# A fused gated-attention and MoE kernel: Q's transposed steps regrouped in runs of 16, masks and output rows to match, and one load untied from the weight conversions

## The chip, the cores and the metric

The kernel runs on one core of one Trainium2 chip. Its time is device microseconds of one launch, from a few runs; smaller is better. The times here are the median of three runs, and the profile is of one further execution.

## The reference

```python
def _attn_ref(q, k, v, a_re, a_im):            # each (B, H, S, D) = (4, 8, 768, 48), float32
    mag = np.sqrt(a_re * a_re + a_im * a_im)
    scale = np.minimum(mag, 0.999) / (mag + 1e-06)
    a_re_n, a_im_n = (a_re * scale, a_im * scale)
    for t in range(S):                         # S_re, S_im: (B, H, D, D), zero at first
        ar, ai = (a_re_n[:, :, t, :, None], a_im_n[:, :, t, :, None])
        new_re = ar * S_re - ai * S_im
        new_im = ar * S_im + ai * S_re
        kv = np.einsum('bhd,bhde->bhde', k[:, :, t], v[:, :, t])   # outer product of k and v
        S_re, S_im = (new_re + kv, new_im)
        y[:, :, t] = np.einsum('bhd,bhde->bhe', q[:, :, t], S_re)

def _moe_ref(x, w_in, w_out):                  # w_in (384, 2048), w_out (2048, 384)
    h = x @ w_in
    r = np.maximum(h, 0.0)
    return ((r * r) @ w_out).astype(np.float32)

# x = y as (B*S, H*D) = (3072, 384); the output is (3072, 384) float32
```

A recurrence with a complex decay for each channel runs along S for each of 32 heads. Its output, with the 8 heads side by side, goes through a two-layer block with a squared relu.

## The kernel before, in words

**Units.** The 4 x 768 tokens are cut into NU = 6 units of L = 512 tokens, each in W = 4 chunks of C = 128 tokens. In a unit the 8 heads are 4 pairs; tile halves z = 0 and 1 hold two pairs each (`aq[z]`, `ff[z]`). The complex values of one head are R = 96 rows, cut in NJ = 3 blocks of 32. In the natural layout partition p holds the four steps 4p to 4p+3 of its chunk, "c" being the step mod 4.

**What a unit does.** `load` (L882, SP's queue, and L896 for v on POOL's) brings a_re, a_im, then q and k. The chain (L913 to L1197: logarithms and roots on ACT from L918 and L926, normalisation on DVE at L929 to L950, running products at L968 and L976, totals over partitions by PE at L997, then the decays applied to q and k at L1155 to L1193) leaves decayed Q and K in `ff[z]`. `gather` (L1230) copies K in natural layout to KC for the state update. For each pair, `turn` (unit 2 on, EARLY = 2) transposes Q and K: two DVE 32x32 block transposes of 128x768 (L1266) write into `aq[z]`, and 12 DMAs (L1271, 8 on SP's queue, 4 on ACT's) move 32-row blocks to the tile QT, where the 96 rows are on partitions. In units 0 and 1 `turn_pe` (L1289) does it with PE and ACT instead. Then come `score` (PE L1314, and DVE L1317 multiplies by the causal mask), `keep` (PE L1343, DVE L1357: the state), `mix` (PE L1369 and L1373 into the accumulator yp, ACT L1381 copies to yt, five DMAs per two pairs at L1388 put yt into xT, the 384 rows of the MoE's input).

**The dense part.** L1410 multiplies xT by w_in, ACT squares the relu (L1441, L1442) or DVE does half of it (L1522), and L1456 (unit 0) or L1507 (later units) multiplies by w_out. L1531 moves the result to the tile `ot`, and `rows` (L1468) writes 128 rows of 384 with one DMA, on POOL's queue, but on SP's for the last two blocks of the last unit.

**Weights.** Both weight matrices arrive as 64-bit patterns in 8 + 8 pieces (`fetch`, L799 on POOL's queue) and are turned into float32 by `convert`: L813 and L817 on ACT, L819, L823 and L826 on DVE. Pieces 3 to 7 of w_in carry the extra key ("a", 1) among the first DVE step's reads.

**Order of the work.** Every operation is a step in the class `Plan` with an engine, a duration written by hand, keys that it reads and writes, and a rank. `Plan.order` schedules the steps in a list over these durations (ready steps first by rank: chain of the next unit, pairs, conversions, dense), and emits them in the order of their planned starts. Each engine and each DMA queue then runs its own instructions strictly in this order. A key that a step reads makes later writers of that key wait for it, too; so the load that next writes ("a", 1), unit 1's second a, is ordered behind those w_in conversions. In the trace the w2 matmuls of the unit before serve as filler among a unit's pairs, and behind a unit's last mix stand those w1 matmuls that need only xT's first rows. The planner's set of engines is iterated in an order that can differ between builds, so that builds of one file can differ in the order of a few steps of unit 0 and 1.

The layout that the change is about: in QT the columns of Q and K are written with

```python
dst = T6[:, i % 2].rearrange("p j (k h t c) -> p k c h j t", k=2, h=2, c=W)
```

so that column t*4 + c is step 4t + c: order of time, every write 4 elements from the one before. `score` and `mix` read and write with matching views.

Of the kernel before, what the change touches and what calls it, by code (L numbers as in the profile page):

```python
# [598 lines left out]
def fast_path(ctx, tc, q, k, v, a_re, a_im, moe_w_in, moe_w_out, out, flag):  # L599
# [98 lines left out]
    for o in range(2):  # L698
        for p0 in (0, CH):
            part = mask[p0:p0 + CH, ts(o, C)]  # L700
            pool.affine_select(out=part, in_=part, pattern=[[1, C]], compare_op=ALU.is_ge,
                               fill=0.0, base=-(p0 ^ (CH * o)), channel_multiplier=-1)
    mask4 = mask.rearrange("p (o t) -> p o t", o=2).unsqueeze(1).to_broadcast([C, W // 2, 2, C])
    dve.memset(ypair, 0.0)
    for b in ("sc0", "sc1"):
        dve.memset(bank[b], 0.0)
# [93 lines left out]
            (CONV, i), 2 * PW * 4 * C, 4.0)  # L800

    def convert(i):
        held = [("a", 1)] if SOON <= i < NPIECE else []
        _, t, keys, dst, n, wk = piece(i)
        t3 = t.rearrange("p m (f two) -> p m f two", two=2)
        lo, hi = t3[:, :, :, 0], t3[:, :, :, 1]
        bits = dst.bitcast(U32)
        rank = (W2, 0.6) if i >= NPIECE else (W1, 0.3)
        def part(dtype, i):
            return t.bitcast(dtype).rearrange("p m (f four) -> p m f four", four=4)[:, :, :, i]  # L810

# [14 lines left out]
        step("DVE", tt(PW), keys + [("lo", i, int(mixed))], wk, lambda: dve.tensor_tensor(  # L826
            out=bits, in0=bits, in1=lo, op=ALU.add), rank)
# [38 lines left out]
    def load(n):  # L866
# [23 lines left out]
        for i in range(W):  # L890
            b, s = divmod(n * L + i * C, S)
            src = v[b, :, s:s + C, :].rearrange("h t d -> t h d")
            for p0, t0, m in places(i):
                vrank = (CHAIN, 1) if n == 1 else (DENSE, 6 + n)
                dma(pool, [("xT", (n - (vs(n) == vs(n - 1))) % 2, NM - 1)] if n else [("gate",)], [("v", vs(n))],
                    lambda i=i, p0=p0, t0=t0, m=m, src=src: pool.dma_start(  # L896
                        out=t[p0:p0 + m, i], in_=src[t0:t0 + m]), vrank, m * 1536, 4.0,
                    group=n)

# [318 lines left out]
    def gather(n, z, p, np):  # L1218
# [5 lines left out]
        for i in needs(n):  # L1224
            for p0, t0, m in places(i):
                queue = sp if n < EARLY and i % 2 else pool
                t0, m4 = 32 * i + t0 // W, m // W
                dma(queue, keys, [(k_, z, q_) for q_ in range(p, p + np)
                                  for k_ in ("KC", "KC%d" % (i == 3))],
                    lambda i=i, p0=p0, t0=t0, m=m, m4=m4, queue=queue: queue.dma_start(  # L1230
                        out=kc[p0:p0 + m, i], in_=nat[t0:t0 + m4]),
                    rank, m * w * 4, group=(n, p))

    slot = {"tr": 0, "sc": 0, "A": 0, "St": 0, "yt": 0, "QT": 0, "d": 0, "ot": 0, "g": 0}
    trs = ["tr0", "tr1"]
# [6 lines left out]
    def pairs(n, which):  # L1244
# [9 lines left out]
        def turn(i):  # L1254
# [2 lines left out]
            t = QT[s].rearrange("p (i x) -> p i x", i=W)  # L1257
            got["T", i] = s
            T6 = aq[z].rearrange("p (y j x) -> p y j x", y=2, j=NJ)
            for j in range(2):  # L1260
                nat = ff[z][:, j * Z:(j + 1) * Z].rearrange(
                    "p (c h j r) -> p c h j r", c=W, h=HH, j=NJ)[:, :, ts(i % 2, 2)]
                dst = T6[:, i % 2].rearrange("p j (k h t c) -> p k c h j t", k=2, h=2, c=W)
                step("DVE", 1.39, [("f", z, 2 * j), ("f", z, 2 * j + 1)],
                     [("a", z) if i % 2 == 0 else ("qk", z)],
                     lambda nat=nat, dst=dst, j=j: dve.transpose(out=dst[:, j], in_=nat), rank)  # L1266
            for b in range(W):
                for j in range(NJ):
                    queue = act if j == 2 else sp
# [26 lines left out]
        def columns(s):  # L1296
            t6 = QT[s].rearrange("p (i k h %s) -> p i k h t c" % "t c",
                                 i=W, k=2, h=2, c=W)[0:R]
            return t6[:, :, 0], QT[s].rearrange("p (i k h t) -> p i k h t", i=W, k=2, h=2)[0:R, :, 1]

        def score(i, h):
            s = got["T", i]
            qt, kt = columns(s)
            b = "sc%d" % take("sc", 2)
            sa = bank[b].rearrange("p (j t c) -> p j t c", j=W, c=W)
# [11 lines left out]
            step("DVE", tt(L), [(b,)], [("A", a)], lambda: dve.tensor_tensor(  # L1317
                out=As[a].rearrange("p (j o t) -> p j o t", o=2, t=C),
                in0=bank[b].rearrange("p (j o t) -> p j o t", o=2, t=C), in1=mask4,
                op=ALU.mult), rank)  # L1320

        def keep(i):
# [35 lines left out]
                                 out=o, in0=ps[:, j], in1=at[j], op=ALU.add), rank)  # L1358

        def mix(i):  # L1360
            qt, _ = columns(got["T", i])
            y4 = ypair.rearrange("p (j t c) -> p j t c", j=W, c=W)
            at, s = got["S", i]
            aa = [As[got["A", i, h]].rearrange("p (j t) -> p j t", j=W) for h in range(2)]

            def go():
                for j in range(W):
# [2 lines left out]
                                  rhs=aa[h][:, j], start=True, stop=at[j] is None)  # L1370
                    for h in range(2):
                        if at[j] is not None:
                            pe.matmul(y4[64 * h:64 * h + D, j], lhsT=at[j][:, h],  # L1373
                                      rhs=qt[:, j, h], start=False, stop=True)
# [90 lines left out]
    def rows(n, grp, i, o):  # L1465
        r = n * L + (2 * grp + i) * C
        queue = sp if n == NU - 1 and grp == 1 else pool
        dma(queue, [("ot", o, 0), ("ot", o, 1)], [], lambda: queue.dma_start(  # L1468
            out=out[r:r + C, :], in_=ots[o]), (DENSE, n), C * DM * 4)

# [226 lines left out]
```

## Time and profile before

| what | us |
|---|---|
| median of 3 runs | 700.21 |
| lowest, highest run | 698.01, 701.38 |
| the profiled execution | 699.64 |
| its span | 697.9 |
| outside the span | 1.74 |

The profile is a page and a trace of one execution. PE is TensorE's matmuls, PEld its weight loads, DVE, ACT, POOL and SP the other engines; a "q" behind a name is that engine's DMA queue or sequencer. A row of a timeline reads: start in us, duration, engine, line of the kernel, operation, output <- inputs, shape, how many merged; in brackets, the idle time of that engine just before and what ended it. Where rows merge several instructions, the duration is from the start of the first to the end of the last. A row of the page's groups reads: busy us and mean ns of one, then idle time before. A row of DMA issues ends with KB and the median us from issue to landing. One L1410 product of 128x512 in the accumulators is 2 x 3 matmuls of 128x256.

### The profile page before, as it was taken

The numbers are of one execution on the slowest core, as the hardware profiler recorded it, in microseconds if no ns is written. First come the engines' busy times: TensorE is split into PE (matmuls) and PEld (weight loads), VectorE is DVE, ScalarE is ACT, GpSimd is POOL, SyncE is SP. The second block draws the span as 40 slices with busy tenths as digits, with TensorE's granted clock in tenths as the row PEclk, the third lists the DMA queues.
The fourth block names the chain that finished last, engine by engine and source line by source line (L and its number), as shares of the span: only waits on it lengthen the run. The fifth ranks groups of instructions, "written<-read, shape, count | busy, mean of one in ns | idle before, by whom it ended". The sixth has DMA issues, their size and how long they took to land.

```text
span 697.9 us, 11865 instructions
## 1 busy us (share of the span) xinstructions
PE 628.0 (90%) x4442; PEld 558.0 (80%) x4442; DVE 559.1 (80%) x1125; ACT 341.6 (49%) x586; POOL 96.4 (14%) x166
## 2 busy tenths in 40 slices
PE   0117999899999999998999999999999999999996
PEld 0006777586788999987998998998999989989996
DVE  6999994789879799676998798998897999428631
ACT  6688727955675163335544436444357351032230
POOL 6301140021100002020021030011030011032200
PEclk9999899999999999999999999999999999999999
DMA  9924278021440005745027662036560034368600
GB/s 282 336 104 98 64 174 255 3 66 28 138 141 13 12 12 127 187 115 117 2 68 169 153 142 60 1 85 177 136 163 10 23 88 113 93 221 302 249 3 27
DMA packets 52067, 79.53 MB, mean 114 GB/s; under 512 B 7744, under 2 KB 35072, under 8 KB 52000
## 3 DMA queue, kind: packets, MB, share of 16 engines
q0 software_dynamic: 11712, 40.90, 19.4%
q1 hardware_dynamic: 36160, 32.79, 18.8%
q10 hardware_dynamic: 4128, 4.98, 2.9%
q8 instruction: 37, 0.61, 0.4%
q14 instruction: 30, 0.25, 0.1%
HBM read 48.76 MB, written 4.72 MB: 77 GB/s over the span
## 4 chain that ended last, share of the span: by engine, by line
PE 78%; DVE 10%; DMA 5%; issue 3%; SPq 2%; ACT 1%; DVEq 0%; ACTq 0%
PE d L1410 31%; PE d L1507 28%; PE sc L1314 4%; PE tr L1343 3%; PE d L1456 3%; PE yp L1369 3%; PE yp L1373 2%; SPq L882 2%; DMA aq<-in_q_dram 1%; DMA aq<-in_a_im_dram 1%; DVE f L1155 1%; DMA aq<-in_k_dram 1%; DVE aq L950 1%; PE tr L997 1%; DMA xT<-yt 1%
## 5 line engine op out<-in xcount | busy, mean ns | idle before, releaser
L1410 PE MATMUL d<-xT,w 128*128 128x256 f32 x1056 | 238.2, 382 | 5.9 <-issue 4.6
L1410 PEld LDWEIGHTS d<-xT,w 128*128 128x128 f32 x1056 | 199.2, 191 | 34.9 <-issue 7.9
L1507 PE MATMUL d<-w,g 128*128 128x192 f32 x832 | 144.2, 328 | 0.0
L1507 PEld LDWEIGHTS d<-w,g 128*128 128x128 f32 x832 | 135.2, 190 | 1.8 <-issue 0.9
L1441 ACT ACTIVATE g<-d 128x512 f32<-128x512 f32 x88 | 52.4, 596 | 128.3 <-PE d L1410 125.3
L1442 ACT ACTIVATE g<-g 128x512 f32<-128x512 f32 x96 | 60.6, 631 | 3.0
L1507 PE MATMUL d<-T,g 128*128 128x192 f32 x336 | 59.6, 328 | 0.0
L1507 PEld LDWEIGHTS d<-T,g 128*128 128x128 f32 x336 | 55.0, 190 | 0.5 <-issue 0.2
L1522 DVE TENSOR_TENSOR g<-g 128x512 f32<-128x512 f32 x56 | 38.1, 690 | 20.5 <-ACT g L1442 13.1
L1230 POOL DMA_DIRECT2D KC<-f x52 | 27.6, 543 | 182.0 <-DVE f L1193 138.9
L1381 ACT COPY yt<-yp 112x512 f32<-112x512 f32 x24 | 14.0, 584 | 73.3 <-PE yp L1373 67.1
L1266 DVE STREAM_TRANSPOSE aq<-f 128x768 f32<-128x768 f32 x32 | 48.3, 1593 | 0.2
L1468 POOL DMA_DIRECT2D out_dram<-ot x22 | 12.3, 561 | 260.0 <-DVE ot L1531 255.9
L1155 DVE TENSOR_TENSOR f<-aq,xn 128x384 f32<-128x384 f32 (+1 forms) x64 | 45.6, 751 | 1.6 <-ACT xn L1106 1.4
L1456 PE MATMUL d<-w,g 128*128 128x384 f32 x128 | 44.1, 491 | 2.2 <-DVE w L826 2.2
L1317 DVE TENSOR_TENSOR A<-sc,mask 128x512 f32<-128x512 f32 x45 | 30.2, 691 | 10.7 <-PE sc L1314 10.5
L968 DVE TENSOR_TENSOR f<-aq 128x384 f32<-128x384 f32 x72 | 37.0, 554 | 0.8
L1314 PE MATMUL sc<-QT 96*64 96x128 f32 (+1 forms) x736 | 37.6, 254 | 0.0
L1456 PEld LDWEIGHTS d<-w,g 128*128 128x128 f32 x128 | 23.4, 190 | 17.6 <-DVE w L826 4.1
L1314 PEld LDWEIGHTS sc<-QT 96*64 96x64 f32 x736 | 34.1, 139 | 4.0 <-issue 3.3
L1531 DVE TENSOR_TENSOR ot<-ot,d 128x192 f32<-128x192 f32 x61 | 20.8, 350 | 18.6 <-PE d L1507 17.9
L997 PE MATMUL tr<-perm,xn 128*128 128x128 f32 x36 | 6.2, 301 | 29.3 <-DVE xn L976 29.3
(179 smaller groups left out, 944.1 us busy)
## 6 DMA issues: line engine op xcount, KB each, us to landing
QT<-aq SPq DMA_DIRECT2D x128, 64.0 KB, 2.0
f<-in_moe_w_in_dram POOLq DMA_DIRECT2D x8, 768.0 KB, 7.1
f<-in_moe_w_out_dram POOLq DMA_DIRECT2D x8, 768.0 KB, 7.2
out_dram<-ot POOLq DMA_DIRECT2D x22, 192.0 KB, 2.6
QT<-aq ACTq DMA_DIRECT2D x64, 64.0 KB, 2.1
KC<-f POOLq DMA_DIRECT2D x36, 96.0 KB, 3.5
xT<-yt SPq DMA_DIRECT2D x36, 96.0 KB, 2.9
aq<-in_a_re_dram SPq DMA_DIRECT2D x8, 384.0 KB, 4.3
```

What stands on the lines that cost most here:

```text
L968: lambda c=c, j=j: dve.tensor_tensor(out=f[j], in0=a[:, :, :, c - 1], in1=a[:, j, :, c].unsqueeze(1).to_broadcast([C, 2, HH, D]), op=ALU.m ...
L1155: lambda j=j, r=r: dve.tensor_tensor(out=f4[:, j, r], in0=a[:, r], in1=over(j), op=ALU.mult), late[z])
L1230: lambda i=i, p0=p0, t0=t0, m=m, m4=m4, queue=queue: queue.dma_start(out=kc[p0:p0 + m, i], in_=nat[t0:t0 + m4]),
L1266: lambda nat=nat, dst=dst, j=j: dve.transpose(out=dst[:, j], in_=nat), rank)
L1314: pe.matmul(sa[p0:p0 + CH, j, t0:], lhsT=kt[:, j, h, ts(half, CH)], rhs=qt[:, j, h, t0:], start=True, stop=True)
L1317: step("DVE", tt(L), [(b,)], [("A", a)], lambda: dve.tensor_tensor(out=As[a].rearrange("p (j o t) -> p j o t", o=2, t=C), in0=bank[b].rear ...
L1410: pe.matmul(ps, lhsT=w1[:, f // FP, m, ts(f % FP, C)], rhs=xT[:, n % 2, m, ts(grp, G)], start=(m == 0), stop=(m == NM - 1))
L1441: act.activation(out=o, in_=ps, func=AF.Relu)
L1442: act.activation(out=o, in_=o, func=AF.Square)
L1456: pe.matmul(ps, lhsT=gt[:, f % 2, ts(i, C)], rhs=w2[:, f], start=(f == 0), stop=(f == NF - 1))
L1507: pe.matmul(bank[b][:, 0:DH], lhsT=g4[:, r, j], rhs=w(j), start=first and j == 0, stop=last and j == NT - 1)
L1522: step("DVE", tt(4 * C), gk(x0, h) + gk(x1, h), gk(o, h), lambda: dve.tensor_tensor(out=g4[:, o, sl], in0=g4[:, x0, sl], in1=g4[:, x1, sl] ...
```

## The change

1. From unit 2 on K is transposed first, as before, in order of time. Q is transposed by two instructions of 128x384, one for each head of the pair, which write the columns of each 128-step chunk in the order (half of the chunk, step mod 4, 16 groups): runs of 16 neighbouring elements. The planned duration of these is that of a 384-element operation (0.47 each), instead of 1.39 for the one.
2. `score` and `mix` take QT's columns as they stand. The score's columns, and the rows of y behind it, are then in the new order from unit 2 on; the shapes and the number of matmuls stay.
3. A second mask, the first with its columns in the new order, is made by one ACT copy of 128x256, and is used from unit 2 on.
4. `rows` undoes the order: from unit 2 on each block of 128 rows goes out in two DMAs of 64 partitions whose DRAM side is the pattern 4 x 16 x 384.
5. `convert` names the steps that last wrote ("a", 1) as something to wait for, and no longer as a read; unit 1's second a load is no longer ordered behind these conversions.
6. v's rank and the gather's source are written differently, with the same result.

```diff
-    mask = sb("mask", 2 * C)
+    masks = sb("mask", 4 * C)
+    mask = masks[:, 0:2 * C]
...
-    mask4 = mask.rearrange("p (o t) -> p o t", o=2).unsqueeze(1).to_broadcast([C, W // 2, 2, C])
+    mask4 = [m.rearrange("p (o t) -> p o t", o=2).unsqueeze(1).to_broadcast([C, W // 2, 2, C])
+             for m in (mask, masks[:, 2 * C:4 * C])]
...
-        held = [("a", 1)] if SOON <= i < NPIECE else []
+        held = tuple(plan.wrote[("a", 1)][1]) if SOON <= i < NPIECE else ()
...
-        step("DVE", ts2(PW), keys + held, wk, lambda: dve.tensor_scalar(
+        step("DVE", ts2(PW), keys, wk, lambda: dve.tensor_scalar(
             out=bits, in0=hi, scalar1=0x07FFFFFF, scalar2=3,
-            op0=ALU.bitwise_and, op1=ALU.logical_shift_left), rank)
+            op0=ALU.bitwise_and, op1=ALU.logical_shift_left), rank, after=held)
...
+    step("ACT", ac(2 * C) + 0.2, [], [("mask",)], lambda: act.copy(
+        out=masks[:, 2 * C:4 * C].rearrange("p (o c t) -> p o t c", o=4, c=W),
+        in_=mask.rearrange("p (o t c) -> p o t c", o=4, c=W)), (CHAIN, 0.2))
...
-            for j in range(2):
+            for j in (1, 0):
                 nat = ff[z][:, j * Z:(j + 1) * Z].rearrange(
-                    "p (c h j r) -> p c h j r", c=W, h=HH, j=NJ)[:, :, ts(i % 2, 2)]
-                dst = T6[:, i % 2].rearrange("p j (k h t c) -> p k c h j t", k=2, h=2, c=W)
-                step("DVE", 1.39, [("f", z, 2 * j), ("f", z, 2 * j + 1)],
-                     [("a", z) if i % 2 == 0 else ("qk", z)],
-                     lambda nat=nat, dst=dst, j=j: dve.transpose(out=dst[:, j], in_=nat), rank)
+                    "p (c h j r) -> p c h j r", c=W, h=HH, j=NJ)
+                ops = [(nat[:, :, ts(i % 2, 2)], T6[:, i % 2].rearrange(
+                    "p j (k h t c) -> p k c h j t", k=2, h=2, c=W)[:, 1])] if j else [
+                    (nat[:, :, 2 * (i % 2) + h], T6[:, i % 2].rearrange(
+                        "p j (k h o c t) -> p k h c j o t", k=2, h=2, o=2, c=W)[:, 0, h])
+                    for h in range(2)]
+                for src, dst in ops:
+                    step("DVE", 1.39 if j else tt(384), [("f", z, 2 * j), ("f", z, 2 * j + 1)],
+                         [("a", z) if i % 2 == 0 else ("qk", z)],
+                         lambda src=src, dst=dst: dve.transpose(out=dst, in_=src), rank)
...
-                            p0, t0 = CH * (half ^ (j % 2)), CH // W * half
-                            pe.matmul(sa[p0:p0 + CH, j, t0:], lhsT=kt[:, j, h, ts(half, CH)],
-                                      rhs=qt[:, j, h, t0:], start=True, stop=True)
+                            p0, t0 = CH * (half ^ (j % 2)), CH * half
+                            pe.matmul(sa[p0:p0 + CH, j, t0:], lhsT=T[:, j, 1, h, t0:t0 + CH],
+                                      rhs=T[:, j, 0, h, t0:], start=True, stop=True)
...
-                            pe.matmul(y4[64 * h:64 * h + D, j], lhsT=at[j][:, h],
-                                      rhs=qt[:, j, h], start=False, stop=True)
+                            pe.matmul(ypair[64 * h:64 * h + D, ts(j, C)], lhsT=at[j][:, h],
+                                      rhs=T[:, j, 0, h], start=False, stop=True)
...
+        if n < EARLY:
+            dma(queue, [("ot", o, 0), ("ot", o, 1)], [], lambda: queue.dma_start(
+                out=out[r:r + C, :], in_=ots[o]), (DENSE, n), C * DM * 4)
+            return
+        for p0 in (0, CH):
+            dma(queue, [("ot", o, 0), ("ot", o, 1)], [], lambda p0=p0: queue.dma_start(
+                out=out[r + p0:r + p0 + CH, :].rearrange("(t c) e -> c t e", c=W),
+                in_=ots[o][p0:p0 + CH]), (DENSE, n), CH * DM * 4)
```

More of the change, by code (lines that the diff above doesn't have):

```diff
@@ L892, in load @@
             src = v[b, :, s:s + C, :].rearrange("h t d -> t h d")
+            vrank = (CHAIN, 1) if n == 1 else (DENSE, 6 + n)
             for p0, t0, m in places(i):
-                vrank = (CHAIN, 1) if n == 1 else (DENSE, 6 + n)
-                dma(pool, [("xT", (n - (vs(n) == vs(n - 1))) % 2, NM - 1)] if n else [("gate",)], [("v", vs(n))],
-                    lambda i=i, p0=p0, t0=t0, m=m, src=src: pool.dma_start(
+                dma(pool, [("xT", (n - (vs(n) == vs(n - 1))) % 2, NM - 1)] if n else [("gate",)],
+                    [("v", vs(n))], lambda i=i, p0=p0, t0=t0, m=m, src=src: pool.dma_start(
                         out=t[p0:p0 + m, i], in_=src[t0:t0 + m]), vrank, m * 1536, 4.0,
@@ L1294, in turn_pe @@
                         group=(n, i))
[L1296 to L1299, printed above, removed]
         def score(i, h):
             s = got["T", i]
-            qt, kt = columns(s)
+            T = QT[s].rearrange("p (i k h t) -> p i k h t", i=W, k=2, h=2)[0:R]
             b = "sc%d" % take("sc", 2)
-            sa = bank[b].rearrange("p (j t c) -> p j t c", j=W, c=W)
+            sa = bank[b].rearrange("p (j t) -> p j t", j=W)
             a = take("A", 3 if 0 < n < ROOM else 2)
@@ L1312, in go @@
                         for j in (j0, j0 + 1):
-                            p0, t0 = CH * (half ^ (j % 2)), CH // W * half
-                            pe.matmul(sa[p0:p0 + CH, j, t0:], lhsT=kt[:, j, h, ts(half, CH)],
-                                      rhs=qt[:, j, h, t0:], start=True, stop=True)
+                            p0, t0 = CH * (half ^ (j % 2)), CH * half
+                            pe.matmul(sa[p0:p0 + CH, j, t0:], lhsT=T[:, j, 1, h, t0:t0 + CH],
+                                      rhs=T[:, j, 0, h, t0:], start=True, stop=True)
             step("PE", SCORE, [("QT", s, h)], [(b,)], go, rank, slack=True)
-            step("DVE", tt(L), [(b,)], [("A", a)], lambda: dve.tensor_tensor(
+            step("DVE", tt(L), [(b,), ("mask",)], [("A", a)], lambda: dve.tensor_tensor(
                 out=As[a].rearrange("p (j o t) -> p j o t", o=2, t=C),
-                in0=bank[b].rearrange("p (j o t) -> p j o t", o=2, t=C), in1=mask4,
+                in0=bank[b].rearrange("p (j o t) -> p j o t", o=2, t=C), in1=mask4[n >= EARLY],
                 op=ALU.mult), rank)
@@ L1360, in mix @@
         def mix(i):
-            qt, _ = columns(got["T", i])
-            y4 = ypair.rearrange("p (j t c) -> p j t c", j=W, c=W)
+            T = QT[got["T", i]].rearrange("p (i k h t) -> p i k h t", i=W, k=2, h=2)[0:R]
             at, s = got["S", i]
```

8 lines of the change are left out of this document (3 added, 5 removed).

## The prediction, made before the changed kernel ran

> **What bounds the kernel now.** I read the page's busy shares first, then its chain of waits, then busy time by stretches of the span, and last the timelines of the few places where TensorE stands still.
>
> ```profile
> span 697.9 us, 11865 instructions
> PE 628.0 (90%) x4442; PEld 558.0 (80%) x4442; DVE 559.1 (80%) x1125; ACT 341.6 (49%) x586; POOL 96.4 (14%) x166
> PE 78%; DVE 10%; DMA 5%; issue 3%; SPq 2%; ACT 1%; DVEq 0%; ACTq 0%
> ```
>
> ```profile
> 0.00:60.00 60.00, 6.50 (x26) 4.96 (x27) 52.98 (x132) 43.53 (x65) 19.08 (x42) 1.00 0.67 214
> 60.00:140.00 80.00, 75.25 (x528) 58.11 (x527) 63.20 (x110) 54.33 (x87) 13.44 (x20) 0.96 0.50 128
> 140.00:318.00 178.00, 173.29 (x1291) 150.49 (x1290) 149.79 (x317) 89.65 (x163) 19.95 (x34) 1.00 0.33 86
> 318.00:612.00 294.00, 294.00 (x2184) 271.74 (x2182) 252.69 (x494) 133.18 (x237) 30.54 (x52) 1.00 0.38 92
> 612.00:698.00 86.00, 78.94 (x424) 72.70 (x420) 40.45 (x75) 20.87 (x35) 13.44 (x19) 0.99 0.45 162
> ```
>
> The second fence's rows are stretch and length, then busy time of PE, its weight load, DVE, ACT and POOL. The chain is 78% PE. From 318 to 612 us PE is busy 294.00 of 294.00 us. In the first 60 us it has nearly nothing to do (6.50), and the change leaves the work of that stretch alone but for a mask copy. So only PE's gaps after 60 us can go: 4.75 + 4.71 + 7.06 = 16.5 us, of which the last 6 us or so are the final output. Each gap has a row in PE's timeline (start, length, what, and in brackets the idle time before it):
>
> ```profile
> 125.92 1.56 PE L1456 MATMUL d<-w,g 128*128 128x384 f32 x4 [0.47 <-DVE w L826]
> 128.35 6.92 PE L1456 MATMUL d<-w,g 128*128 128x384 f32 x20 [0.88 <-DVE w L826]
> 137.39 2.85 PE L1456 MATMUL d<-w,g 128*128 128x384 f32 x8 [0.83 <-DVE w L826]
> ...
> 306.47 1.57 PE L1507 MATMUL d<-w,g 128*128 128x192 f32 x8
> 307.88 1.03 PE L1410 MATMUL d<-xT,w 128*128 128x256 f32 x4
> ...
> 310.73 1.99 PE L1410 MATMUL d<-xT,w 128*128 128x256 f32 x8
> 317.36 7.88 PE L1410 MATMUL d<-xT,w 128*128 128x256 f32 x29 [4.63 <-issue]
> ...
> 612.19 2.94 PE L1410 MATMUL d<-xT,w 128*128 128x256 f32 x12
> 616.09 6.28 PE L1410 MATMUL d<-xT,w 128*128 128x256 f32 x28 [0.96 <-DMA xT<-yt]
> ```
>
> These are the three waits for converted pieces of w_out (2.18 us together), the end of unit 2 (4.63) and the end of unit 5 (0.96).
>
> **The change part by part.** *The transposes.* The group of L1266 holds 4 units x 4 pairs x (Q, K); in order of time four of them take 5.83 us, 1.46 each.
>
> ```profile
> L1266 DVE STREAM_TRANSPOSE aq<-f 128x768 f32<-128x768 f32 x32 | 48.3, 1593 | 0.2
> 264.56 5.83 DVE L1266 STREAM_TRANSPOSE aq<-f 128x768 f32<-128x768 f32 x4
> 104.42 1.02 DVE L968 TENSOR_TENSOR f<-aq 128x384 f32<-128x384 f32 x2
> ```
>
> Each of the 16 for Q becomes two of 384 elements that write runs of 16. No such transpose is in the trace. If it ran at the rate of now with one more start, two would take 1593 ns or a little more, a loss of 0.1 to 0.2 us per Q; if it ran like the L968 pair of the same 384 elements, 1.02 us, a gain of 0.44. I take the gain, since only the written pattern differs: 16 x 0.44 = 7.0 us of DVE. At 318 to 612 DVE is busy 252.69 of 294 us under a PE without a gap, so this saves nothing by itself. What it changes is the plan's order, since the planned cost falls from 1.39 to 0.94. (The Trainium skill, "Vector Engine (DVE) Microarchitecture Reference", section 5.2, says that a write of single words with a step costs 1.71 to 2.5 ns per column and runs of two or more words 1.05; 1593 ns for 768 is 2.07 ns, which agrees, and by it two transposes would be estimated at 0.95 us.)
>
> *The order at the end of unit 2.* The instruction order of the changed kernel has the last mix 8 w2 matmuls earlier, and behind it 8 w2 matmuls (L1507) and 12 w1 matmuls that need only old xT, where now 8 stand. From the last mix's end (310.73) to the landing (317.36) are 6.63 us. Filler now is 1.99; then it is 1.41 (306.47 to 307.88) + 2.94 (the row at 612.19) = 4.35. Idle: 6.63 - 4.35 = 2.28 instead of 4.63, **-2.35**. Bounds: 0, if the landing comes as much later; -4.63, if it takes the 3.90 us of unit 5 (612.19 to 616.09).
>
> *The order at the end of unit 5.* There the opposite: 4 of the 12 w1 matmuls move ahead of the last mix. Filler falls from 2.94 to 1.99, **+0.95** (bounds 0 and 0.95). In units 3 and 4 the fillers change by a few matmuls and still exceed 6.63 us: 0.
>
> *The untied load.* Unit 1's second a stands behind all xT on SP's queue now, and ACT's L926 waits for its stream:
>
> ```profile
> 85.91 7.70 SPq L1388 DMA_DIRECT2D xT<-yt  x5
> 93.65 1.53 SPq L882 DMA_DIRECT2D aq<-in_q_dram  x2
> 95.23 1.27 SPq L882 DMA_DIRECT2D aq<-in_k_dram  x2
> 96.60 1.30 SPq L882 DMA_DIRECT2D aq<-in_a_re_dram  x2
> 98.00 1.25 SPq L882 DMA_DIRECT2D aq<-in_a_im_dram  x2
> ```
>
> ```profile
> 119.13 1.48 ACT L926 ACTIVATE f<-aq 128x1536 f32<-128x1536 f32 x1 [2.20 <-DMA aq<-in_k_dram]
> 82.13 0.55 DVE L1193 TENSOR_TENSOR f<-aq 128x384 f32<-128x384 f32 x1
> 103.54 0.96 DVE L826 CUSTOM_DVE_ANT_0 w<-T,w 128x1536 uint16<-128x1536 uint16 x1
> 111.08 2.75 PE L1410 MATMUL d<-xT,w 128*128 128x256 f32 x12
> ```
>
> ```profile
> 91.85 0.59 ACT L1381 COPY yt<-yp 112x512 f32<-112x512 f32 x1 [3.60 <-PE yp L1373]
> 100.06 0.60 ACT L1441 ACTIVATE g<-d 128x512 f32<-128x512 f32 x1 [7.63 <-PE d L1410]
> ```
>
> ```profile
> 91.53 1.75 DVE L950 TENSOR_TENSOR aq<-aq,f 128x1536 f32<-128x1536 f32 x1
> ```
>
> Its buffer is last read at 82.7 (L1193), so a_re can be issued then, ahead of the first xT, and a_im behind the first three xT, near 88. The four issues move past xT's last two, which wait for their copy until 92.4, so xT loses nothing. L926 then runs ahead of the first relus instead of at 119; its 2.20 us wait and 1.48 us of work leave the stretch where ACT and DVE convert w_out, and so do L931 to L938 and DVE's L929 to L950. The three PE waits, each under 0.9 us, then go: **-2.18** (bounds -2.18, and +2 if others come). What it displaces: up to four DVE steps of 768 elements (1.02 each by the two of L968) and L950's 1.75, 5.8 us in all, now stand between w1's conversions. The last of these ends at 104.5 and would end at 110.3; it serves the last 12 matmuls, which start at 111.08. So the cover is 0.8 us more than what it has to hide; without it PE would stand for up to 5.8.
>
> *The mask copy.* One ACT copy of 128x256, the fourth on ACT's queue:
>
> ```profile
> 5.36 0.84 ACT L918 ACTIVATE f<-aq 128x768 f32<-128x768 f32 x1 [3.27 <-DMA aq<-in_a_re_dram]
> ```
>
> ACT waits 3.27 us there for a load; the copy of 256 elements fits in (768 take 0.84), 0. Without the cover: up to 0.84.
>
> *The output rows.* 16 of the DMAs become 32 of 96 KB, 28 on POOL, which is 14% busy, and 4 on SP, of which the last two follow the last w2 matmul.
>
> ```profile
> 691.94 0.35 DVE L1531 TENSOR_TENSOR ot<-ot,d 128x192 f32<-128x192 f32 x1 [2.25 <-PE d L1507]
> L1468 SPq DMA_DIRECT2D out_dram<-ot x2: 350/361/372, 689.7 to 692.3; - x2
> ```
>
> ```profile
> KC<-f POOLq DMA_DIRECT2D x36, 96.0 KB, 3.5
> xT<-yt SPq DMA_DIRECT2D x36, 96.0 KB, 2.9
> out_dram<-ot SPq DMA_DIRECT2D x2, 192.0 KB, 3.0
> ```
>
> A second issue is 0.36; a 96 KB piece lands in 2.9 to 3.5 us where the 192 KB one needs 3.0. I take 0.36 + 0.25 = **+0.6** (bounds 0.26 and 0.86 by these rows). On POOL 14 more issues wait for nothing that PE waits for: 0.
>
> *The rest* (score and mix reading contiguous columns, the gathers' precomputed source) keeps every instruction and shape: 0.
>
> **Sum.** -2.35 + 0.95 - 2.18 + 0.6 = -2.98, so 699.64 for the profiled execution (1.74 outside its span) becomes 696.66. The median of the runs, 700.21, lies 0.57 above that execution; the forecast for the median is **697.2**, 0.43% less. About 0.5% (3.5 us) is what a measurement of this kernel can tell from no change.
>
> **The rivals.**
>
> *All of xT's wait shortens.* Unit 2's last xT lands 6.63 us after the mix although unit 5 needs 3.90, because v, q and k loads follow on its heels. If in the new order it gets ahead of them, the other 2.28 go, and with 0.95 at unit 5 covered the time is 694.0. For: DVE is freed of 7 us, so what the loads wait for comes earlier or later than the mix, not beside it. Against: v is released by the same mix. Chance 0.22, 692.5 to 695.5.
>
> *Slower: unit 1's second a blocks ACT.* L926 now stands ahead of the first relus of unit 0, and DVE's L929 ahead of w1's later conversions. In the stretch from 78 to 112 us loads took long:
>
> ```profile
> aq<-in_a_im_dram SPq DMA_DIRECT2D x2, 192.0 KB, 20.1
> ```
>
> If a_im issued near 88 took 20.1 us, it would land at 108, L926 and four steps of 768 elements (0.84 to 1.02 each, 5.2 us in all) would end at 113, and the first relu would come 13 us later than now, when it runs at 100.06. PE has seven accumulators' worth of w1 matmuls, about 1.3 us each, ahead, so it would stand some 9 us: 706. It decides from a landing after about 99. Against: these two were issued after 98 into a full DMA system; here nothing queues before 93.65. Chance 0.12, 702 to 710.
>
> *Split outputs are slow.* (The Trainium skill, "DMA: Bandwidth & Descriptors", section "Why a DMA increments its semaphore by 16 and not by 1", says that a DMA is spread over the largest number of engines up to 16 that divides both patterns' slowest dimension. The new DRAM pattern is 4x16x384, so 4 engines. No row of before shows such a pattern.) As a mechanism here: the page's best slice moves 336 GB/s on 16 engines, 21 each; 98 KB on 4 takes 1.17 us instead of 0.29, and the last two on the same 4 engines 2.34 instead of 0.58, so the tail costs 0.36 + 1.76 = 2.1 instead of 0.6, and one xT behind an output up to 1.2 more: 698.7 to 700. Chance 0.13.
>
> ```profile
> GB/s 282 336 104 98 64 174 255 3 66 28 138 141 13 12 12 127 187 115 117 2 68 169 153 142 60 1 85 177 136 163 10 23 88 113 93 221 302 249 3 27
> ```
>
> *The transposes get no faster*, the change doesn't do what it says: two take 1.6 to 1.7, the plan counts 0.94, and scores stand up to 0.7 us too early in PE's queue, 16 times. With half of them uncovered +5.6: 702.8. Chance 0.05.
>
> **How the numbers follow.** My forecast, 695.5 to 699, has 0.48, of which 0.13 lies under 696.7. Faster: 0.22 + 0.13 = 0.35. Slower (over 703.7): 0.12, 0.03 of the last rival and 0.02 for what isn't listed, 0.17. The same: 0.48. The range, 692.5 to 704.5, leaves out most of the blocked ACT and little else.
>
> **What would show it.** Transposes: L1266 x48, 32 of them near 0.5 us. Unit 2: one idle row of about 2.3 us before L1410 near 313; unit 5: 1.9. L926's second run before 95, and no wait for L826 in PE's rows near 130; if its row stands at 100 or later with PE idle near 105, the slower rival is right. Tail: 6.6 us from the last w2 matmul to the end instead of 6.0; 7.5 speaks for few engines. PE's busy sum should stay at 628 within 1 us; if it doesn't, the sum is wrong at its root.

## The result, and the profile after

The changed kernel takes 693.38 us (median of 10 runs, 690.51 to 695.59) against 699.13 (10 runs, 697.57 to 702.55): the ratio is 0.991, with a 95% interval of 0.989 to 0.993. It is faster by 0.8 to 0.9%, 5.75 us between the medians. The profiled execution is 691.44 us with a span of 689.7 (699.64 and 697.9 before). The two profiled executions lie 8.2 us apart and the medians 5.75, since the changed kernel's profile is the second fastest of its ten; the accounts below are of the two profiles.

The page of the changed kernel, its span, busy shares and chain:

```profile
span 689.7 us, 11895 instructions
PE 624.4 (91%) x4442; PEld 556.1 (81%) x4442; DVE 550.6 (80%) x1141; ACT 340.5 (49%) x587; POOL 107.4 (16%) x180
PE 85%; DVE 10%; DMA 2%; issue 1%; ACT 0%; SPq 0%; DVEq 0%; ACTq 0%
```

The span lost 8.2 us. PE's idle time went from 697.9 - 628.0 = 69.9 to 689.7 - 624.4 = 65.3, 4.6 less; the other 3.6 are PE's busy time, though it runs the same 4442 matmuls. So there are two things to find: waits that went, and matmuls that became faster.

The waits first. Counts of matmuls are the trace's, which records each of the kernel's as two (the 9 matmuls added in one experiment below stand there as x18). PE's timeline of the changed kernel at the ends of units 2 and 5 (L1415 is the old L1410, L1518 the old L1507):

```profile
303.04 1.57 PE L1518 MATMUL d<-w,g 128*128 128x192 f32 x8
304.44 10.52 PE L1415 MATMUL d<-xT,w 128*128 128x256 f32 x48
314.80 0.27 PE L999 MATMUL tr<-perm,xn 128*128 128x128 f32 x1
315.24 0.76 PE L999 MATMUL tr<-perm,xn 128*128 128x128 f32 x5 [0.17 <-DVE xn L978]
...
606.72 5.63 PE L1415 MATMUL d<-xT,w 128*128 128x256 f32 x25 [1.84 <-DMA xT<-yt]
```

Unit 2's wait of 4.63 us is gone: 48 w1 matmuls run in one piece. Unit 5's has grown from 0.96 to 1.84. The three waits near 130 us are gone too. Here is the stretch in the changed kernel, w2 of unit 0 being L1461 now:

```profile
92.08 1.13 PE L1415 MATMUL sc<-xT,w 128*128 128x256 f32 x4 [0.18 <-DVE w L828]
93.64 1.13 PE L1415 MATMUL sc<-xT,w 128*128 128x256 f32 x4 [0.43 <-DVE w L828]
95.22 1.97 PE L1415 MATMUL d<-xT,w 128*128 128x256 f32 x8 [0.45 <-issue]
...
111.70 16.93 PE L1461 MATMUL d<-w,g 128*128 128x384 f32 x52
128.47 0.82 PE L999 MATMUL tr<-perm,xn 128*128 128x128 f32 x6
129.12 4.04 PE L1461 MATMUL d<-w,g 128*128 128x384 f32 x12
```

The end got longer. The last add ends at 682.92, the span at 689.7, so 6.8 us against 697.9 - 692.29 = 5.6 before. In the rows of DMA issues, the pieces of half the size land later on POOL's queue, in 3.9 us, than whole rows do (192 KB are units 0 and 1 here, 2.4; in before 2.6):

```profile
out_dram<-ot POOLq DMA_DIRECT2D x28, 96.0 KB, 3.9
out_dram<-ot POOLq DMA_DIRECT2D x8, 192.0 KB, 2.4
```

The last add, and SP's queue at the end:

```profile
682.57 0.35 DVE L1542 TENSOR_TENSOR ot<-ot,d 128x192 f32<-128x192 f32 x1 [2.25 <-PE d L1518]
680.35 3.71 SPq L1478 DMA_DIRECT2D out_dram<-ot  x4
```

Of the last line's issues, with the shortest, median and longest duration in ns,

```profile
L1478 SPq DMA_DIRECT2D out_dram<-ot x4: 523/552/695, 680.3 to 683.5; - x4
```

one takes 552 ns, where it took 361. SP's queue is through with its issues at 684.06, 1.14 us after the last add, where in before it was 0.38 (692.67). So 0.76 of the 1.17 us are issue, and 0.41 are what follows it. Idle in sum: -4.46 - 2.18 + 0.88 + 1.17 - 0.15 (waits near 95 us) = -4.7, which is the 4.6 counted above.

Now the faster matmuls. Stretches of one microsecond behind unit 2's stall, in the kernel before; the number after the five engines' busy times is the clock that was granted to PE:

```profile
317.00:318.00 1.00, 0.64 (x2) 0.58 (x3) 0.96 (x2) 0.00 (x0) 0.00 (x0) 0.50 1.09 233
318.00:319.00 1.00, 1.00 (x4) 0.82 (x3) 1.00 (x1) 0.00 (x0) 0.00 (x0) 0.50 1.12 275
319.00:320.00 1.00, 1.00 (x3) 0.78 (x3) 0.96 (x3) 0.00 (x0) 0.00 (x0) 0.50 1.13 199
320.00:321.00 1.00, 1.00 (x6) 0.84 (x5) 0.93 (x4) 0.26 (x1) 0.00 (x0) 0.92 1.09 245
```

PE works at half its clock for 3 to 4 us after the stall. The 29 matmuls of the row at 317.36, quoted in the prediction, take 7.88 us; at the pace of the 48 in 10.52 they would take about 6.4, so the stall cost some 1.6 us more than its idle row shows. A second slow stretch lies in unit 0:

```profile
75.00:80.00 5.00, 4.38 (x46) 3.99 (x48) 4.69 (x9) 4.49 (x10) 0.00 (x0) 0.78 0.32 78
80.00:85.00 5.00, 5.00 (x46) 4.43 (x42) 4.24 (x9) 2.00 (x4) 1.09 (x2) 0.54 0.36 79
```

In the changed kernel's profile both windows are at 1.00. From the end of PE's wait for KC at 75.61 to the end of its first wait for a piece of w_in at 94.20, before takes 18.6 us; the changed kernel takes 16.6 (75.48 to 92.08). These 2.0 and the 1.6 behind unit 2's stall are about the 3.6 us of busy time. Four of the experiments below have before's order on PE there and a clock of 1.00, and take 15.95 to 16.1 us for the same way (planned cost alone: 76.35 to 92.30), so the stretch costs about 2.5.

### The profile page after: what moved, and what is told of

Read it like the earlier page. It is cut to its first block, busy times and chain, and to the rows that moved or that the text cites. A ratio compares the mean times of both kernels' runs of the same rounds, so it can differ in the third digit from the quotient of the medians.

```text
span 689.7 us, 11895 instructions
## 1 busy us (share of the span) xinstructions
PE 624.4 (91%) x4442; PEld 556.1 (81%) x4442; DVE 550.6 (80%) x1141; ACT 340.5 (49%) x587; POOL 107.4 (16%) x180
## 4 chain that ended last, share of the span: by engine, by line
PE 85%; DVE 10%; DMA 2%; issue 1%; ACT 0%; SPq 0%; DVEq 0%; ACTq 0%
PE d L1415 31%; PE d L1518 28%; PE d L1461 6%; PE sc L1320 5%; PE tr L1349 4%; PE yp L1374 3%; PE yp L1378 2%; PE tr L1415 2%; PE sc L1415 1%; DVE f L970 1%; PE tr L1300 1%; DMA aq<-in_a_im_dram 1%; DVE aq L952 1%; PE tr L999 1%; DMA xT<-yt 1%; PE d L1300 1%
## 5 line engine op out<-in xcount | busy, mean ns | idle before, releaser
L1415 PE MATMUL d<-xT,w 128*128 128x256 f32 x1056 | 234.9, 380 | 2.3 <-DMA xT<-yt 1.8
L1415 PEld LDWEIGHTS d<-xT,w 128*128 128x128 f32 x1056 | 198.9, 190 | 30.1 <-issue 3.6
L1518 PE MATMUL d<-w,g 128*128 128x192 f32 x832 | 144.6, 329 | 0.0
L1518 PEld LDWEIGHTS d<-w,g 128*128 128x128 f32 x832 | 135.2, 190 | 2.7 <-issue 1.7
L1518 PE MATMUL d<-T,g 128*128 128x192 f32 x336 | 59.4, 328 | 0.0
L1518 PEld LDWEIGHTS d<-T,g 128*128 128x128 f32 x336 | 54.9, 190 | 0.6 <-issue 0.4
L1461 PE MATMUL d<-w,g 128*128 128x384 f32 x128 | 44.4, 493 | 0.0
L1478 POOL DMA_DIRECT2D out_dram<-ot x28 | 17.9, 642 | 161.8 <-DVE ot L1542 129.8
L1277 DVE STREAM_TRANSPOSE aq<-f 128x384 f32<-128x384 f32 (+1 forms) x48 | 39.4, 898 | 0.2
L1461 PEld LDWEIGHTS d<-w,g 128*128 128x128 f32 x128 | 23.4, 190 | 14.0 <-issue 0.2
```

What stands on the lines that cost most here:

```text
L1277: lambda src=src, dst=dst: dve.transpose(out=dst, in_=src), rank)
L1415: pe.matmul(ps, lhsT=w1[:, f // FP, m, ts(f % FP, C)], rhs=xT[:, n % 2, m, ts(grp, G)], start=(m == 0), stop=(m == NM - 1))
L1461: pe.matmul(ps, lhsT=gt[:, f % 2, ts(i, C)], rhs=w2[:, f], start=(f == 0), stop=(f == NF - 1))
L1518: pe.matmul(bank[b][:, 0:DH], lhsT=g4[:, r, j], rhs=w(j), start=first and j == 0, stop=last and j == NT - 1)
```

## The experiments

All builds have the planner's engines in a written order, because the set's order of iteration can move steps of unit 0: one order for most, and its reverse in the whole output rows, the order alone (both runs) and the quick transposes in the same order, which gives unit 0 the order of the profiled changed kernel. The runs are three series on three chips, and ratios are to runs of the kernel before in the same series. I set three theories against each other: **order** (the lower planned cost of Q's transposes changes PE's order, and that closes the stall), **speed** (quicker transposes do) and **load** (the untied load does).

**The untied load alone.**

```diff
-        held = [("a", 1)] if SOON <= i < NPIECE else []
+        held = tuple(plan.wrote[("a", 1)][1]) if SOON <= i < NPIECE else ()
...
-        step("DVE", ts2(PW), keys + held, wk, ...
+        step("DVE", ts2(PW), keys, wk, ..., rank, after=held)
```

> The kernel before with the untied load alone; the planner's set of engines is a fixed list here, as in all experiments, so that builds agree. Order theory (what Q's lower planned cost does to PE's order gives the gain in units 2 to 5, the untied load that in units 0 and 1): the three waits for L826 (2.2 us) go, the wait at the end of unit 2 (4.6) stays: about 697, ratio 0.997. Load theory (the untied load is the whole gain): 693 to 694, ratio 0.992. Speed theory (the quicker transposes are the gain): 699, ratio 1.000. If the low granted clock that the profile of before shows from 75 to 85 us belongs to the tied load, it is gone here.

Measured: 699.78 us, ratio 0.998 (0.995 to 1.001). Its timeline on PE:

```profile
89.35 1.19 PE L1410 MATMUL d<-xT,w 128*128 128x256 f32 x2 [1.71 <-DMA xT<-yt]
98.89 3.10 PE L1410 MATMUL d<-xT,w 128*128 128x256 f32 x8 [1.95 <-DMA xT<-yt]
317.10 9.70 PE L1410 MATMUL d<-xT,w 128*128 128x256 f32 x36 [4.43 <-issue]
```

The waits for L826 did go, but two waits for xT, 3.66 us, took their place: in this order of unit 0 a pair of w1 matmuls stands ahead of the last mix, and the a loads go out beside the xT that it needs. The granted clock falls to 0.50 behind both (in windows from 89.4 to 92.7 and from 99.6 to 102.9 us). Near 78 us it is 1.00 here, which by itself would fit the tied load as the cause of the low stretch; the run with the load tied again, below, speaks against that. The load theory is out as the whole cause.

**The planned cost alone**: K first and 0.94 written for Q, one slow transpose of Q as before.

```diff
-            for j in range(2):
+            for j in (1, 0):
...
-                step("DVE", 1.39, [("f", z, 2 * j), ("f", z, 2 * j + 1)],
+                step("DVE", 1.39 if j else 0.94, [("f", z, 2 * j), ("f", z, 2 * j + 1)],
```

> The kernel before with K's transpose ahead of Q's and Q's planned at 0.94 instead of 1.39 us; every instruction as before, one 768-element transpose of about 1.59 us for Q as well, whole output rows. PE's order from unit 2 on is that of the changed kernel. Order theory: unit 2's wait falls by 4 to 4.5 us, unit 5's rises by 0.9, transposes that are slower than planned cost little: 695.5 to 696, ratio 0.995. Speed theory: scores come 0.65 us late per pair against the plan, and nothing else changes: 699 to 704, ratio 1.000 to 1.007. Load theory: 699, ratio 1.000.

Measured: 694.42 us, ratio 0.991 (0.988 to 0.994). With Q's slow transpose and whole output rows, one number in the planner and K's place ahead of Q give what the whole change gives. Unit 2's end in its timeline:

```profile
306.55 1.57 PE L1507 MATMUL d<-w,g 128*128 128x192 f32 x8
307.96 10.52 PE L1410 MATMUL d<-xT,w 128*128 128x256 f32 x48
```

**All but the untied load**: the changed kernel with the first diff's two places set back.

> The changed kernel with the load tied to the conversions again (a read of the key, as before). Order theory: the waits for L826 near 130 us are back (+2.2 against the changed kernel), unit 2's wait stays away: 695.5 to 696, ratio 0.995. Load theory: 699 or slower by the split output rows, ratio 1.000 to 1.002. Speed theory: 693 to 694, ratio 0.992. If the low clock from 75 to 85 us belongs to the tied load, it is back.

Measured: 697.35 us, ratio 0.993 (0.990 to 0.996). The waits for L826 are back (L828 here), unit 2's stall is not:

```profile
128.27 1.56 PE L1461 MATMUL d<-w,g 128*128 128x384 f32 x4 [0.70 <-DVE w L828]
130.71 6.92 PE L1461 MATMUL d<-w,g 128*128 128x384 f32 x20 [0.88 <-DVE w L828]
139.75 2.85 PE L1461 MATMUL d<-w,g 128*128 128x384 f32 x8 [0.83 <-DVE w L828]
...
312.31 10.52 PE L1415 MATMUL d<-xT,w 128*128 128x256 f32 x48
```

So the stall doesn't hang on the load. The ratio fits the order theory's 0.995; the time is 1.4 us over its 696. In this profile the clock near 78 us is 1.00 with the load tied, so the tied load alone doesn't halve it.

**The old planned cost** in the changed kernel: quick transposes without the order.

```diff
-                    step("DVE", 1.39 if j else tt(384), ...
+                    step("DVE", 1.39 if j else 0.695, ...
```

> The changed kernel with the two transposes of Q planned at 0.695 each (1.39 together, as the one before): quick transposes and the untied load, but a PE order that the lower cost didn't make; the last mix of unit 2 is then followed by w1 matmuls alone, 12 of them before xT is needed, and unit 5's end keeps the order of before. Order theory: unit 2's wait is 6.6 - 2.9 = 3.7 us, unit 5's 0.96, the split rows cost 1.2 at the end, the untied load gives 2.2: about 697, ratio 0.997. Speed theory and load theory: as the changed kernel, 693 to 694, ratio 0.992.

Measured: 699.74 us, ratio 0.999 (0.996 to 1.003). With the untied load and all of DVE's saving, but another order, nothing is left:

```profile
88.75 0.67 PE L1415 MATMUL d<-xT,w 128*128 128x256 f32 x2 [1.55 <-DMA xT<-yt]
96.44 1.97 PE L1415 MATMUL d<-xT,w 128*128 128x256 f32 x8 [1.70 <-issue]
311.55 6.71 PE L1415 MATMUL d<-xT,w 128*128 128x256 f32 x30 [2.99 <-issue]
```

The order theory holds, speed falls. My 697 was too low, since the two waits near 90 us came here as well. Behind none of the three waits does this profile show a clock under 1.00.

**The gap filled with idle work.** Unit 2's last mix is followed by 9 matmuls whose result nothing reads:

```diff
+                if n == 2 and i == 3:
+                    for x in range(9):
+                        pe.matmul(bank["tr0"][0:C, 0:2 * C], lhsT=ident, rhs=w1[:, 0, 0], start=True, stop=True)
```

> The kernel before, with 9 matmuls of 128x256 on idle data (3.9 us) into an unused accumulator right behind the last mix of unit 2: they shorten no wait for xT, they only keep TensorE busy through most of it. Clock theory (a stall of 4.6 us also halves the granted clock for the 3.5 us behind it, which costs about 1.6 us of slower matmuls): the granted clock after the stall stays at 1.00, the first 29 w1 matmuls behind it take 6.4 instead of 7.9 us, and the time falls by about 1.6 us, ratio 0.998. Rival (the low clock behind the stall is a chance of single executions, or has another cause): 0.50 is there again, ratio 1.000.

Measured: 696.03 us, ratio 0.993 (0.990 to 0.996). TensorE works through the wait for nothing, and the kernel is faster. A window behind the wait, and the added matmuls (L1377) with w1's rows:

```profile
317.00:318.00 1.00, 1.00 (x6) 0.90 (x5) 1.00 (x2) 0.97 (x2) 0.00 (x0) 1.00 1.07 212
```

```profile
308.50 4.15 PE L1377 MATMUL tr<-w,ident 128*128 128x256 f32 x18
312.49 1.89 PE L1413 MATMUL d<-xT,w 128*128 128x256 f32 x8
314.75 8.01 PE L1413 MATMUL d<-xT,w 128*128 128x256 f32 x36 [0.38 <-issue]
```

In before the same 36 matmuls stand in one row as

```profile
317.36 9.39 PE L1410 MATMUL d<-xT,w 128*128 128x256 f32 x36 [4.63 <-issue]
```

so 1.4 of the expected 1.6 us are gone with the low clock. The time fell by more (the interval reaches from 3.2 to 7.0 us). The stretch near 78 us is missing in this profile, which is worth about 2.5 (75.99 to 91.96 instead of 75.61 to 94.20), and by their mean clock of 0.998 or more 6 of the 8 executions lack it.

**v behind xT.** A small POOL copy that reads unit 2's xT holds unit 3's v loads back.

```diff
+        hold = []
+        if n == 3:
+            hold = [("gate", n)]
+            step("POOL", 0.2, [("xT", (n - 1) % 2, m) for m in range(NM)], hold,
+                 lambda: pool.tensor_copy(out=gate[:, 0:NM], in_=xT[:, (n - 1) % 2, :, L - 1]), (DENSE, 6 + n))
```

> The kernel before, with unit 3's six v loads held back by a small POOL copy that reads unit 2's xT, so that they are issued only when xT has landed; PE's order as before. Landing theory (in before v loads go out beside the last xT and double its landing; the changed order puts an output DMA ahead of v on POOL's queue, and xT gets through): xT lands in 2.3 to 2.8 instead of 4.6 us, the stall at unit 2's end falls from 4.6 to about 2.3, and with it goes the low clock behind it (1.6): 4 us in all, ratio 0.994 to 0.995. Rival (only the filler order shortened the stall, q and k delay xT as much as v): stall 4.2 to 4.6 still, ratio 1.000.

Measured: 695.00 us, ratio 0.990 (0.987 to 0.993), at the order of before. The last xT lands in 2.4 us (5.2 in before), the wait is 1.79, and the clock behind it is 1.00. Some of it is paid back: PE waits 1.50 us for unit 3's chain at 325.50, which it doesn't in before.

```profile
316.00 0.75 POOL L893 COPY gate<-xT 128x3 f32<-128x3 f32 x1 [5.35 <-DMA xT<-yt]
316.69 4.54 POOL L901 DMA_DIRECT2D v<-in_v_dram  x6
```

```profile
315.89 8.01 PE L1415 MATMUL d<-xT,w 128*128 128x256 f32 x36 [1.79 <-DMA xT<-yt]
```

Compare the rows of before and of the changed kernel, which did the same without meaning to. In before the output DMA was out at 308.73 and v followed on the mix; in the changed kernel the mix ends at 303.0 but the output's add only frees the queue at 305.29, and v stands behind it. First before, POOL's timeline and the row of xT's issues in that window with KB and the median us to landing (the two of before took 4.0 and 5.2), then the same of after:

```profile
309.60 4.53 POOL L896 DMA_DIRECT2D v<-in_v_dram  x6 [0.32 <-PE yp L1373]
```

```profile
xT<-yt SPq DMA_DIRECT2D x2, 96.0 KB, 4.6
```

```profile
305.29 0.54 POOL L1474 DMA_DIRECT2D out_dram<-ot  x1 [17.41 <-DVE ot L1542]
305.85 4.52 POOL L898 DMA_DIRECT2D v<-in_v_dram  x6
```

```profile
xT<-yt SPq DMA_DIRECT2D x2, 96.0 KB, 2.3
```

So unit 2's wait is the time from the last mix to xT's landing, less the filler: 6.63 - 1.99 in before, 3.79 - 1.99 with v held back, 5.86 - 2.86 with the old planned cost. In the changed kernel xT lands some 3.7 us after the mix (the last is issued at 304.3), and the filler of 4.35 covers that. Neither half closes the wait alone: the longer filler would have left 2.28, the earlier landing left 1.79.

**Whole output rows**: ACT's copy undoes the order, and each block of 128 rows is one DMA again. This and the next kernel have the order of unit 0 that the profiled changed kernel has.

```diff
+            if n >= EARLY:
+                ysrc = ysrc.rearrange("p (b c t) -> p b t c", b=2 * W, c=W)
+                ydst = ydst.rearrange("p (b t c) -> p b t c", b=2 * W, c=W)
```

> The changed kernel, but ACT's copy of yp to yt puts y back into order of time from unit 2 on, so that every 128 output rows go out in one DMA as before. If the split outputs cost what the profile of the changed kernel shows at its end (6.8 us from the last add to the end instead of 5.6): -1.2 us there, and the permuted copy (0.58 us plain, perhaps 0.9 so) costs up to 0.3 at the end of unit 5: about 692.5, ratio 0.990 to 0.989. If they also held up other transfers: 691 or less. If they cost nothing: 693 to 694, ratio 0.992.

Measured: 691.21 us, ratio 0.985 (0.981 to 0.989), the end 689.9 - 684.57 = 5.3 us, 1.5 less than the changed kernel's. The ratio fell by more than that, but the two kernels were timed in different series, so whether split rows cost more than the end stays open. The permuted copy is free; its group, 16 permuted and 8 plain, has the 583 ns of the changed kernel's plain ones:

```profile
L1391 ACT COPY yt<-yp 112x512 f32<-112x512 f32 x24 | 14.0, 583 | 61.4 <-PE yp L1378 61.4
684.22 0.35 DVE L1541 TENSOR_TENSOR ot<-ot,d 128x192 f32<-128x192 f32 x1 [2.25 <-PE d L1517]
```

**The order alone**: before's instructions, Q planned at 0.94 in units 2 to 4 and 1.39 in unit 5, and the untied load.

> Every instruction of the kernel before: one 768-element transpose for Q, one mask, whole output rows. Only the order differs: Q planned at 0.94 in units 2 to 4 (1.39 in unit 5), K first, and the untied load with the order of unit 0 that the profiled changed kernel has. Order theory: unit 2's stall and its low clock go, unit 5 waits 0.96 instead of 1.8, no waits for L826 near 130, the end as before: 690.5 to 692, ratio 0.986 to 0.988, and so faster than the changed kernel. Speed theory: no better than 697.

Measured: 690.25 us, ratio 0.983 (0.980 to 0.987): faster than the changed kernel, with none of its quicker transposes.

**The kernel before, once more.**

> The kernel before with the planner's engines in the fixed order that gives the profiled kernel's order: the measure for all other runs. Ratio 1.000, some 700 us, and a mean granted clock of 0.988 to 0.997 in each execution. If the clock of before is lower only because of what follows unit 2's stall, no execution should be above 0.997; and if the low stretch near 78 us depends on chance alone, it should be missing in as many executions as in kernels without that stall (about 3 of 4).

Measured: 698.90 us, ratio 0.997 (0.995 to 1.000), clocks from 0.989 to 0.996. So a difference of 0.3% between two series of one program is within what these ratios carry. None is above 0.997, as expected. The low clock near 78 us is in this profile too, and 3 of 12 executions are at 0.996; in the kernels without unit 2's stall, 7 of 8 with the planned cost alone, 7 of 8 with v behind xT and 6 of 8 with the gap filled were at 0.996 or more. Since the stall alone lowers the mean, this count can't say how often the stretch near 78 is missing, and chance alone is neither shown nor ruled out.

**The untied load in the other order of unit 0** was not what ran.

> Placeholder name for the kernel before with the untied load alone, now with the other order of unit 0 (the one that the profiled changed kernel has: the last mix of unit 0 ahead of the first w1 matmuls, all w2 matmuls behind the last of w1). In the first run of this edit PE waited 1.7 and 2.0 us for xT near 89 and 97 us. If these waits belong to the order of unit 0, they are gone here, the three waits for L826 too, and the time is 2 to 3 us under before: ratio 0.996. If they belong to the untied load as such (its transfers beside xT's), they stay: ratio 0.999 to 1.001.

Measured: 699.12 us, ratio 0.997 (0.994 to 1.000). This kernel is the very one of the first experiment, so the run repeats it: waits of 1.88 and 2.39 for xT again, and no gain. Whether the other order of unit 0 is enough to make the load worth its 2.2 us was not tried by itself. The changed kernel has that order, and waits only 0.45 there.

**Quick transposes in the same order**: whole rows, Q planned at 1.39 in unit 5, beside **the order alone again**. On PE the two have the same order.

> The changed kernel with whole output rows (ACT's copy puts y back in order of time) and Q's planned cost in unit 5 at 1.39: quick transposes, and on PE exactly the order of the next kernel. Order theory: the 9 us that DVE saves lie under a busy PE, so the same as the next kernel within 1 us: ratio 0.983 to 0.985. Speed theory: 3 us or more faster than the next: 0.979 or less.

> The kernel of the run that had every instruction of before in the order of the changed one (slow transposes for Q, planned at 0.94 in units 2 to 4; untied load), run again beside the one that differs only in the quick transposes: ratio 0.983 to 0.985 again.

Measured: 688.06 us, ratio 0.982 (0.979 to 0.985), and 689.06 us, ratio 0.985 (0.981 to 0.988). DVE's 7 us less busy (551.8 and 558.8) are worth about 1 us, not told apart from nothing. The first is the fastest kernel of this study, by the medians 5 us under the changed one, which was timed in another series.

## Why the prediction was right, and where not

The range held the time, and the sign was right. The size was not: 2.98 us forecast, 5.75 measured. By the sign that I had set for myself, PE's busy sum at 628 within 1 us, the sum was wrong at its root: it fell by 3.6, and no term of mine was about the clock. By the terms:

- **Transposes, 0 on the path: right.** The groups of the changed kernel, by shape:

```profile
L1277 DVE STREAM_TRANSPOSE aq<-f 128x768 f32<-128x768 f32 x16 | 25.3, 1581 | 0.2
L1277 DVE STREAM_TRANSPOSE aq<-f 128x384 f32<-128x384 f32 x32 | 16.5, 557 | 0.0
```

  Two take 1.11 us instead of 1.59. DVE was 8.5 us less busy, with 7.0 forecast, and the last pair of kernels shows what that is worth.
- **The planned cost moves PE's order: right, and it is the cause**, by the planned cost alone, the old planned cost and the last pair of kernels.
- **Unit 2, -2.35: the mis-sized term.** It measured -4.46 of idle and about -1.6 of slow clock, 6 us in all. The filler was as worked out; two things were missing. The landing was held at 6.63 us from the mix, and fell to some 3.7 because v went out later; I had that as a rival with 0.22, but argued it from DVE and not from POOL's queue, where it happened. That its 694.0 lies within 0.6 of the median is partly luck: it took unit 5's 0.95 as covered, which came (+0.88), and has no term for the slow clock. And I had priced a stall by its idle row alone, though the row behind it, 7.88 us for 29 matmuls, stood in my own quotes. The Trainium skill has the rule ("TensorE: Matmul & The Clock Gate", section "Why this matters for your kernels"): no idle gaps of PE over about 3 us between bursts of matmuls, or the clock is halved. The traces agree: the clock was 0.50 behind gaps of 4.3 to 4.8 us, and 1.00 behind one of 2.99. But the untied load's run also shows 0.50 behind waits of 1.71 and 1.95 us, so in a sparsely filled stretch a shorter gap was enough.
- **The untied load, -2.18: right in the profile, with a condition.** L926's second run (L928 now) stands at 91.27 instead of 119.13, and the three waits went:

```profile
91.27 1.49 ACT L928 ACTIVATE f<-aq 128x1536 f32<-128x1536 f32 x1 [1.53 <-DMA aq<-in_a_im_dram]
```

  But in another order of unit 0 the same load gave it all back as waits for xT. I had written that xT loses nothing; of the two orders tried, that held in the one where no w1 matmul stands ahead of the mix.
- **Unit 5, +0.95: right** (+0.88).
- **The end, +0.6: too small** (+1.17; the whole rows take 1.5 off). Both halves of the term were low: the issues added 0.76 and not 0.36, since each takes 0.55, and what follows them 0.41 and not 0.25. The Trainium skill's rule ("DMA: Bandwidth & Descriptors", section "Why a DMA increments its semaphore by 16 and not by 1") that the prediction weighed, by which fewer engines move the split rows, is neither shown nor refuted: on POOL's queue the pieces landed later, 3.9 us against 2.4 to 2.6, but the end grew by 1.17 and not by the 2.1 that I had worked out from it, and no run shows which engines moved them.
- **The slower rival** didn't come: a_im had landed by 91 us, before the 99 at which it would decide. Its price was misread as well: a product of 1.3 us counts six rows of the trace, but the trace has twelve for one, 2.75 us in the row at 111.08, so PE had some 19 us of w1 matmuls ahead and not 9, and the 9 us that this rival priced are too many.

What stays open: why PE's clock near 78 us was at half in both profiles of before and in that of whole output rows, and not in the other kernels, several of which have before's very order on PE up to 270 us. Some of the measured gains over 4 us contain it. Between 75 and 680 us five of the fourteen profiles have stretches at half clock, and each is 3.4 us long or twice that (77.8 to 84.6 and 316.7 to 320.2 in before); within a profile their starts lie whole multiples of 3.4 us apart (89.3, 99.6 and 318.0 with the untied load alone). So here the clock looks as if it is set in steps of 3.4 us, and whether the same short wait halves it may depend on how it lies to these steps. That was not tested.

A second difference lies between executions of one kernel. PE comes up to its full pace at one of two times: in the order alone and the order alone again, one kernel, the 32 score matmuls of unit 0 took 2.83 and 1.56 us:

```profile
61.63 2.83 PE L1314 MATMUL sc<-QT 96*64 96x128 f32 x32
61.12 1.56 PE L1314 MATMUL sc<-QT 96*64 96x128 f32 x32
```

The wait for KC then ends at 78.22 and 74.40, 3.8 us apart. PE came up late in four of the fourteen profiles (v behind xT, all but the untied load, and the untied load's second run are the others), but not in before's nor in the changed kernel's. So single profiles of one kernel can differ by 4 us from this alone, and medians of six or eight executions can shift by part of it.

## What to carry to other kernels

Where a planner writes the order, a change's planned cost is a change of its own; run it without the change. Price a stall of TensorE by its idle row and by the matmuls behind it, and look at what other queues issue in the microsecond in which the awaited transfer goes out. A permutation is cheapest in an instruction that already copies the data.

## What the runs showed of the hardware

A copy from the accumulator by ACT that permutes 512 columns in groups of four by sixteen takes 583 ns, as the plain one does. Idle matmuls in a wait of 4.6 us brought the granted clock behind it from 0.50 to 1.00. Six v loads issued beside the last two xT transfers of a unit made these land in 4.0 and 5.2 us; held back, they let them land in 2.3 to 2.4. Stretches at half clock lasted 3.4 or 6.8 us. The same 32 score matmuls at the start took 1.56 us in one execution of a kernel and 2.83 in another, and PE's next wait ended 3.8 us later.
